# A planned two-stage kernel: scalar loads behind a pair's values, three loads in halves, a weight cast on GpSimd, and a new order

## The chip, the core and the metric

The kernel runs on one core of a Trainium2 chip. The core has TensorE (PE), which multiplies matrices out of SBUF into PSUM, VectorE (DVE), ScalarE (ACT), GpSimd (POOL) and SyncE (SP). Each takes its instructions in the order in which the program gave them; SP's queue here holds nothing but transfers. The metric is the time of one execution on the device in microseconds (us), as the median of several runs; less is better.

## What is computed

Two stages follow each other. The first is a gated linear recurrence over 768 steps, for 4 batches of 8 heads of width 48:

```
for t in range(S):
    state = alpha[:, :, t, :, None] * state + einsum('bhd,bhe->bhde', k[:, :, t], v[:, :, t])
    y[:, :, t] = einsum('bhd,bhde->bhe', q[:, :, t], state)
```

Its output, laid out as x with 3072 rows of 384, goes through a two-layer network with 2048 hidden columns:

```
h = x @ w_in;  r = maximum(h, 0);  g = s * (r * r) + b;  out = g @ w_out
```

s and b are single numbers. All inputs and the output are float32; the kernel multiplies in bf16. Since b is the same for every hidden column, its part of the output is one row (b times the column sums of w_out), computed once as bias_w.

## The kernel before

**Blocks.** The 768 steps of each batch are cut into 6 blocks of 128, 24 blocks in all (n = 0 to 23). The first four are worked as two *pairs*, whose two blocks are loaded interleaved into space that later holds hidden activations (gt); each other block has its own a, q, k and v tile, in five slots (`n % NIN`). The chain of a block: load alpha, q, k, v (192 KB each; `load`, L225); logarithm of alpha on ACT (L381; pairs L552); cumulative sum as a matmul with a triangle of ones (L387, L394; pairs L559, L569); exponentials of it and of its negative on ACT (L403, L406; pairs L578, L583); q times the first and k times the second on DVE (L417, L422; pairs L590); both transposed, for pairs by PE (L605) with a copy out of PSUM by DVE (L616), for later blocks by a transposing transfer that ACT issues (`st_Tdma`, L439); A, the matmul of the two (L490); the causal mask on DVE (L499); y out of A, v and the state (L528); y evacuated by ACT into xd (L673). Beside it the state: v cast to bf16 on POOL (L411; pairs L621), KV (L448; pairs L655), the state's sum on DVE (L469, L473), its decay on POOL (L484). For a pair, half of each block's values lies on the wrong 64 partitions; PE shifts them (L631) and two copies per pair put them in place (`pair_vcopy`, L644).

**The network.** Blocks are taken in groups of one or two (GROUPS). A unit is a piece of the first layer that fills one PSUM bank (mm1, L693: 6 matmuls of 256 columns or 12 of 128, w_in as weights), then relu on ACT (L702) and a square on DVE into gt (L708). A quad is four of the sixteen matmuls that make a block's output (mm2, L755). The last quad of a block is followed by `oevac` on DVE (L766: times s, plus bias_w) and the output store (`ostore`, L779).

**Weights.** w_in and w_out come in four parts each of 768 KB (L310, L333), are cast to bf16 by the engine that the list CE names (L319 on ACT, L321 on DVE, L323 on POOL), and DVE sums w_out's columns (L343, L348, L351). b and s are loaded by POOL (`load_bs`, L359, L360); b is first read by `bias_mul` (L363, "bones"), s by `oevac`.

**What sets the order.** Nothing is ordered by hand and nothing by the framework: the class Schedule holds every operation with its engine, a guessed duration, a priority and what it reads and writes, plays them through once while the program is built, and emits them in the order in which they begin there. On each engine, among the operations that are ready, the one with the least priority value goes first; P holds one offset for each kind of operation, UNIT and LEAD turn a block's number into a base. LOADS gives the order of the first transfers in SP's queue. [...] FILL matmuls on zeros (L1028) are put where this play leaves PE idle before the first quad. So one constant changed can move any instruction on any engine; the hardware keeps the order, and waits by semaphores for what an instruction reads.

Of the kernel before, what the change touches and what calls it, by code (L numbers as in the profile page):

```python
# [14 lines left out]

VW = 144

GROUPS = [2, 2, 1, 1, 1, 1, 2, 2, 2, 2, 2, 2, 2, 2]
UNIT = 0.392
LEAD = {1: 204.6, 2: 323.1, 4: 100.0}  # L20

NPE = 4

NAY = 12

# [6 lines left out]
TP = 1.45  # L32
LATE = 2.5
NY = 2
NKV = 7
NR2 = 2
STQ = 18
TC2 = ["DVE", "DVE"]
VC2 = ["ACT", "ACT"]
CE = ["POOL", "DVE", "ACT", "ACT", "ACT", "ACT", "ACT", "ACT"]  # L40
TC = dict(ACT=1.4, DVE=0.87, POOL=2.0)
FILL_GAP = 0.2
COLD = 9.0

P_BM, P_CS, P_BMM = -5, -286.4, 473.5
P = dict(
    ln=34.88, cum=-15.29, eb=-32.24, ei=9.49, vc=73.43, qb=-9.65, kb=14.71, T=95.62,
    Tc=-13.62, KV=-13.54, t1=9.55, sn=124.73, Ay=-11.39, A=-22.53, mk=-58.68, y=-13.83,
    ye=5.65, m1=-19.67, re=9.86, sq=-33.02, m2=-18.25, oe=-24.3, vm=-57.17, ci=324.52,
    co=-825.8, ls=148.33, vn=-450.01,  # L50
)

LOADS = ["V0", "i0", "A0", "K0", "Q0", "A1", "V1", "Q1", "i1", "K1", "i2", "i3", "v4", "o0", "o1", "o2", "o3", "a4", "k4", "q4"]

class Schedule:
    HOP = 0.05
# [90 lines left out]
def kernel(  # L147
# [12 lines left out]
    nc = tc.nc  # L160
    ctx.enter_context(tc.manual_schedule())

    B, H, S, D = q.shape
    C = 128
# [7 lines left out]
    NIN = 5  # L172
# [31 lines left out]
    a_in = many("a_in", NIN, [128, H, D], FP32)  # L204
# [17 lines left out]

    def load(n, src, dst):
        b, c = n // NCH, n % NCH
        nc.sync.dma_start(  # L225
            out=dst[n % NIN],
            in_=src[b, :, c * C : (c + 1) * C, :].rearrange("h s d -> s h d"),
        )

    for x, src in enumerate((alpha, q, k, v)):  # L230
        load_pair(0, x, src)
# [62 lines left out]
    out_sb = many("o_sb", 3, [128, d_model], FP32)  # L294
# [368 lines left out]
    blk_group = []  # L663
    for g, m in enumerate(GROUPS):
        blk_group += [(g, t) for t in range(m)]
# [11 lines left out]
    quads = []  # L677
    for g, m in enumerate(GROUPS):
        per = 4 // m
        for u in range(NJ // per):  # L680
            units.append((g, [u * per + i for i in range(per)]))
        for tt in range(m):
            for jq in range(NJ // 4):
                quads.append((g, tt, jq))
    first_blk = [sum(GROUPS[:g]) for g in range(len(GROUPS))]

    def mm1(w):
        g, js = units[w]
        n = GROUPS[g] * C
        hp = h_ps[w % 2]  # L690
# [126 lines left out]
    for rank, item in enumerate(loads):  # L817
        t, i = rank - 1000, int(item[1:])
        if item[0] in "AQKV":
            if i == 1:  # L820
                load_pair_op(item[0], i)
            continue
        if item[0] in "aqkv":
            if i < N1 + NIN:
                load_op(item[0], i)
            continue
        st = stage
        stage += 1
        key = [("wst", st)]
        if st >= NST:  # L830
            h = (st - NST) // 2 % 2
            key = [("gt", x, j) for x in range(9 - 3 * h, 12 - 3 * h) for j in range(NJ)]
            key = key[24 * (st % 2) : 24 * (st % 2) + 24] + [("wst", st)]
        if st >= NST:
            reuse.append((len(sched.ops), [(x, h) for x in ("AQ", "KV")[st % 2]]))
        eng = CE[st]
        if item[0] == "i":
            op("SP", TW, t, load_w_in, i, st, w=key, lat=2.0)
            op(eng, TC[eng], P["ci"], cast_w_in, i, st, eng, r=key, w=[("wib", i)], lock=eng != "ACT")
        else:  # L840
            op("SP", TW, t, load_w_out, i, st, w=key, lat=2.0)
            op(eng, TC[eng], P["co"], cast_w_out, i, st, eng, r=key, w=[("wob", i)], lock=eng != "ACT")
# [12 lines left out]
    def pb(n):  # L855
        return "ct" if n >= NKV else "py"

# [106 lines left out]
    def add_group(g):  # L964
        nonlocal unit_i, quad_i
        if g == 0:
            op("PE", 0.65, P_BMM, bias_mm, r=["bones", "colsum"], w=[("o", 0)], lat=0.16)
            op("DVE", 0.53, -300, bias_copy, r=[("o", 0)], w=["bias"])
        m = GROUPS[g]
        ring = [(first_blk[g] + x) % RING for x in range(m)]  # L970
        per = 4 // m
        for u in range(NJ // per):
            w = unit_i
            unit_i += 1
            js = units[w][1]
            t = w * UNIT
            op("PE", {1: 0.67, 2: 0.656, 4: 0.648}[m], t + P["m1"], mm1, w,
               r=[("xd", g % 3, x) for x in range(m)] + [("wib", js[0] // 4)],
               w=[("h", w % 2)], lat=0.16)
            op("ACT", 0.52, t + P["re"], relu, w, r=[("h", w % 2)], w=[("r", w % 2)])  # L980
            op("DVE", 0.345, t + P["sq"], square, w, r=[("r", w % 2)],
               w=[("gt", x, j) for j in js for x in ring], lock=True)
        for u in range(4 * m):
            x = quad_i
            quad_i += 1
            tt, jq = quads[x][1:]
            if x >= len(quads) - 4:
                continue
            ob = (x // 4) % 2
            t = (x + 4 * m + P["m2"]) * UNIT  # L990
            op("PE", 0.65, t, mm2, x,
               r=[("gt", ring[tt], j) for j in range(4 * jq, 4 * jq + 4)] + [("wob", jq)],
               w=[("o", ob)], lat=0.16)
# [69 lines left out]
```

## Time and profile before

| | us |
|---|---|
| median of 7 runs (186.11 to 188.29) | 186.62 |
| the profiled execution's own time | 187.21 |
| its span, first to last instruction | 185.4 |
| busy in the span: PE, DVE, ACT, POOL | 174.0, 135.0, 106.4, 39.5 |
| groups: mm1 matmuls (672), mm2 matmuls (368) | 74.4, 69.4 |
| groups: relu (96), squares (96), masks (24) | 55.4, 42.5, 29.3 |

The profiled execution is one of the seven, 0.6 us above their median; 1.8 us of it lie outside the span. The mean granted clock of PE is 0.991 of full. The DMA engines move 35.48 MB, most of it in packets under 512 bytes, and are full nearly throughout the first three quarters of the span. A busy PE is not the same as a PE at its peak, since the ends of matmuls are modelled and overlap; so what PE waits for is read from its idle time and from what ended it.

### The profile page before, as it was taken

The numbers are of one execution on the slowest core, as the hardware profiler recorded it, in microseconds if no ns is written. First come the engines' busy times: TensorE is split into PE (matmuls) and PEld (weight loads), VectorE is DVE, ScalarE is ACT, GpSimd is POOL, SyncE is SP. The second block draws the span as 40 slices with busy tenths as digits, with TensorE's granted clock in tenths as the row PEclk, the third lists the DMA queues.
The fourth block names the chain that finished last, engine by engine and source line by source line (L and its number), as shares of the span: only waits on it lengthen the run. The fifth ranks groups of instructions, "written<-read, shape, count | busy, mean of one in ns | idle before, by whom it ended". The sixth has DMA issues, their size and how long they took to land.

```text
span 185.4 us, 5345 instructions
## 1 busy us (share of the span) xinstructions
PE 174.0 (94%) x2149; PEld 124.0 (67%) x2151; DVE 135.0 (73%) x251; ACT 106.4 (57%) x215; POOL 39.5 (21%) x71
## 2 busy tenths in 40 slices
PE   6878987999999999999989999999999899999993
PEld 2346764766877667776667776787777677777562
DVE  2389999899498778769769986879788586554321
ACT  3437898874637555675257666585648365665000
POOL 7994032031012221211203230100232130010000
PEclk9999997999999999999999999999999999999999
DMA  5999998999999999999999999799997983000122
GB/s 155 355 315 368 354 378 242 202 193 223 215 193 202 186 160 276 175 219 221 226 183 241 170 226 216 173 203 166 237 142 160 182 172 66 0 11 34 54 77 85
DMA packets 119961, 35.48 MB, mean 191 GB/s; under 512 B 113232, under 2 KB 118352, under 8 KB 119936
## 3 DMA queue, kind: packets, MB, share of 16 engines
q1 hardware_dynamic: 98688, 29.70, 71.2%
q10 hardware_dynamic: 21120, 5.25, 20.8%
q8 instruction: 17, 0.28, 0.7%
q0 software_dynamic: 128, 0.20, 0.3%
q14 instruction: 8, 0.07, 0.1%
HBM read 25.17 MB, written 4.72 MB: 161 GB/s over the span
## 4 chain that ended last, share of the span: by engine, by line
PE 55%; DMA 17%; DVE 16%; issue 4%; ACT 3%; SPq 1%; POOL 1%; ACTq 1%; DVEq 0%; POOLq 0%
PE h_ps L693 21%; PE o_ps L755 21%; DMA v_in<-in_v_dram 9%; DMA qkT<-qk 3%; PE py_ps L528 3%; DVE gt L708 3%; DVE am L499 3%; DMA out_dram<-o_sb 3%; PE a_ps L490 3%; DMA gt<-in_alpha_dram 2%; DVE colpart L343 2%; DVE o_sb L766 2%; ACT r L702 2%; DVE s_st L473 1%; DVE qk L422 1%
## 5 line engine op out<-in xcount | busy, mean ns | idle before, releaser
L693 PE MATMUL h_ps<-xd,w_in_bf 128*128 128x256 bf16 (+1 forms) x672 | 74.4, 260 | 0.8 <-ACT r L702 0.8
L702 ACT ACTIVATE r<-h_ps 128x512 bf16<-128x512 f32 x96 | 55.4, 601 | 29.9 <-PE h_ps L693 11.7
L755 PE MATMUL o_ps<-w_out_bf,gt 128*128 128x384 bf16 x368 | 69.4, 328 | 1.4 <-ACT w_out_bf L319 1.3
L693 PEld LDWEIGHTS <-w_in_bf 128*128 128x128 bf16 x672 | 56.7, 98 | 11.4 <-issue 1.6
L708 DVE TENSOR_TENSOR gt<-r 128x512 bf16<-128x512 bf16 x96 | 42.5, 458 | 15.9 <-ACT r L702 15.4
L755 PEld LDWEIGHTS <-gt 128*128 128x128 bf16 x368 | 34.4, 98 | 20.4 <-issue 1.7
L499 DVE TENSOR_TENSOR am<-a_ps,mask 128x1024 bf16<-128x1024 f32 x24 | 29.3, 1220 | 3.1 <-PE a_ps L490 2.8
L411 POOL CAST vp<-v_in 128x384 bf16<-128x384 f32 x20 | 11.5, 575 | 68.2 <-DMA v_in<-in_v_dram 62.8
L484 POOL TENSOR_TENSOR s_st<-s_st,blast 128x384 bf16<-128x384 bf16 x16 | 14.0, 874 | 43.0 <-DVE s_st L473 30.9
L766 DVE SCALAR_TENSOR_TENSOR o_sb<-o_ps,s_col,bias_w 128x384 f32<-128x384 f32 x23 | 14.2, 616 | 8.8 <-PE o_ps L755 7.9
L673 ACT ACTIVATE xd<-py_ps 128x384 bf16<-128x384 f32 x22 | 11.1, 503 | 12.4 <-PE py_ps L528 12.3
L381 ACT ACTIVATE la<-a_in 128x384 bf16<-128x384 f32 x20 | 10.5, 524 | 7.8 <-DMA a_in<-in_alpha_dram 3.1
L417 DVE TENSOR_TENSOR qk<-q_in,b_s 128x384 bf16<-128x384 f32 x20 | 12.6, 632 | 2.6 <-DMA q_in<-in_q_dram 1.6
L473 DVE TENSOR_TENSOR s_st<-ct_ps,s_st 64x192 bf16<-64x192 f32 x24 | 8.5, 354 | 7.0 <-PE ct_ps L448 4.3
L403 ACT ACTIVATE b_s<-ct_ps 128x384 f32<-128x384 f32 x20 | 9.8, 491 | 5.5 <-PE ct_ps L394 3.9
L422 DVE TENSOR_TENSOR qk<-k_in,binv 128x384 bf16<-128x384 f32 x20 | 11.0, 549 | 0.4 <-DMA k_in<-in_k_dram 0.4
L490 PE MATMUL a_ps<-qkT 64*128 64x128 bf16 x192 | 9.5, 218 | 1.5 <-DMA qkT<-qk 0.8
L490 PEld LDWEIGHTS <-qkT 64*128 64x128 bf16 x192 | 5.6, 94 | 7.7 <-issue 5.4
L406 ACT ACTIVATE binv<-ct_ps 128x384 f32<-128x384 f32 x20 | 9.9, 494 | 0.0
L1028 PE MATMUL o_ps<-zeros 128*128 128x512 bf16 x19 | 7.7, 550 | 1.3 <-DVE zeros L236 1.3
L528 PE MATMUL py_ps<-am,vp 128*32 128x128 bf16 x352 | 8.8, 219 | 0.0
L528 PEld LDWEIGHTS <-vp 128*32 128x32 bf16 x384 | 6.5, 97 | 0.7 <-issue 0.3
(93 smaller groups left out, 124.5 us busy)
## 6 DMA issues: line engine op xcount, KB each, us to landing
out_dram<-o_sb SPq DMA_DIRECT2D x22, 192.0 KB, 3.3
v_in<-in_v_dram SPq DMA_DIRECT2D x20, 192.0 KB, 4.6
a_in<-in_alpha_dram SPq DMA_DIRECT2D x20, 192.0 KB, 4.5
k_in<-in_k_dram SPq DMA_DIRECT2D x20, 192.0 KB, 4.9
q_in<-in_q_dram SPq DMA_DIRECT2D x20, 192.0 KB, 4.7
wst<-in_moe_w_in_dram SPq DMA_DIRECT2D x4, 768.0 KB, 7.1
gt<-in_moe_w_out_dram SPq DMA_DIRECT2D x4, 768.0 KB, 10.0
gt<-in_alpha_dram SPq DMA_DIRECT2D x2, 384.0 KB, 4.6
```

The source lines that it names most:

```text
L411: nc.gpsimd.tensor_copy(out=vp_sb[n % 4].rearrange("a p (x d) -> a p x d", d=D)[:, :, 0:3:2, :], in_=v_in[n % NIN].rearrange("a (p e) d -> ...
L417: nc.vector.tensor_tensor(out=qk_sb[n % 4][:, 0, :, 0:D], in0=q_in[n % NIN], in1=b_sb[n % 2], op=ALU.mult)
L422: nc.vector.tensor_tensor(out=qk_sb[n % 4][:, 1, :, 0:D], in0=k_in[n % NIN], in1=binv_sb[n % 2], op=ALU.mult,)
L484: nc.gpsimd.tensor_tensor(out=s_sb[n % 3], in0=t1_sb[n % 2], in1=bl, op=ALU.mult)
L490: nc.tensor.matmul(out=a_ps[:, e, p, :], lhsT=qkT[64 * e : 64 * e + 64, 1, p, :], rhs=qkT[64 * e : 64 * e + 64, 0, p, :], start=True, stop ...
L499: nc.vector.tensor_tensor(out=am_sb[n % 2].rearrange("a e p t -> a (e p) t"), in0=a_ps.rearrange("a e p t -> a (e p) t"), in1=(mask2 if n ...
L528: nc.tensor.matmul(out=y_of(n)[32 * (x % 4) : 32 * (x % 4) + 32, x // 4, :], lhsT=(st[:, p, c0 : c0 + 32] if e is None else vp[:, p, c0 + ...
L693: nc.tensor.matmul(out=hp[:, i * n : (i + 1) * n], lhsT=w_in_bf[:, kk, 128 * j : 128 * (j + 1)], rhs=xd_sb[g % 3][:, kk, 0:n], start=(kk = ...
L702: nc.scalar.activation(out=r_sb[w % 2], in_=h_ps[w % 2], func=AF.Relu)
L708: nc.vector.tensor_tensor(out=gt_sb[:, s0 : s0 + m, js[0] : js[0] + len(js)].rearrange("a s j t -> a j s t"), in0=r, in1=r, op=ALU.mult,)
L755: nc.tensor.matmul(out=op[:, 0:d_model], lhsT=gt_sb[:, s0, j], rhs=w_out_bf[:, j, :], start=(j == 0), stop=(j == NJ - 1),)
L766: nc.vector.scalar_tensor_tensor(out=ots, in0=o_ps[(x // 4) % 2][:, 0:d_model], scalar=s_col, in1=bias_w, op0=ALU.mult, op1=ALU.add,)
```

## The change

1. For the planner `load_bs` now reads ("V", 1) as well. In the emitted order POOL's two small loads come behind the four value casts of the second pair; before they stood ahead of the first pair's.
2. `load` takes q, k and v of block 20 in two transfers of four heads (96 KB) each.
3. CE: the first w_in part is cast by ACT (was POOL), the fourth by POOL (was ACT); the second stays with DVE.
4. VC2: all four copies of `pair_vcopy` go to DVE (were on ACT).
5. STQ is gone: block 18's output store is issued by SP like the others (was POOL).
6. LOADS: k4 comes ahead of the last two w_in parts, v4 between w_out's second and third part (v4 was ahead of all of w_out, k4 behind it).
7. [...] The groups of one are now blocks 4, 5, 8 and 11 (were 4, 5, 6 and 7); NKV = 8 puts KV of block 7 in the bank that y uses (was ct). NPE decides nothing, since blocks below 4 are pairs.

Counted in the emitted order, the matmuls are the same but for the filling ones, 28 for 21. DVE has the four copies more, ACT has them less; POOL has one store less, SP one store and three loads more.

```
-GROUPS = [2, 2, 1, 1, 1, 1, 2, 2, 2, 2, 2, 2, 2, 2]
-UNIT = 0.392
-LEAD = {1: 204.6, 2: 323.1, 4: 100.0}
+GROUPS = [2, 2, 1, 1, 2, 1, 2, 1, 2, 2, 2, 2, 2, 2]
+UNIT = 1.077
+LEAD = {1: 168.0, 2: 386.1, 4: 142.5}
...
-NKV = 7
+NKV = 8
...
-STQ = 18
-VC2 = ["ACT", "ACT"]
-CE = ["POOL", "DVE", "ACT", "ACT", "ACT", "ACT", "ACT", "ACT"]
-TC = dict(ACT=1.4, DVE=0.87, POOL=2.0)
+VC2 = ["DVE", "DVE"]
+CE = ["ACT", "DVE", "ACT", "POOL", "ACT", "ACT", "ACT", "ACT"]
+TC = dict(ACT=1.43, DVE=1.7, POOL=1.44)
...
-LOADS = ["V0", "i0", "A0", "K0", "Q0", "A1", "V1", "Q1", "i1", "K1", "i2", "i3", "v4", "o0", "o1", "o2", "o3", "a4", "k4", "q4"]
+LOADS = ["i0", "K0", "V0", "A0", "Q0", "A1", "V1", "Q1", "i1", "K1", "k4", "i2", "i3", "o0", "o1", "v4", "o2", "o3", "a4", "q4"]
...
-        nc.sync.dma_start(
-            out=dst[n % NIN],
-            in_=src[b, :, c * C : (c + 1) * C, :].rearrange("h s d -> s h d"),
-        )
+        parts = 2 if n == 20 and dst is not a_in else 1
+        for x in range(parts):
+            hs = slice(H // parts * x, H // parts * (x + 1))
+            nc.sync.dma_start(
+                out=dst[n % NIN][:, hs],
+                in_=src[b, hs, c * C : (c + 1) * C, :].rearrange("h s d -> s h d"),
+            )
...
-        eng = nc.gpsimd if n == STQ else nc.sync
-        eng.dma_start(out=out[n * C : (n + 1) * C, :], in_=out_sb[(x // 4) % 3])
+        nc.sync.dma_start(out=out[n * C : (n + 1) * C, :], in_=out_sb[(x // 4) % 3])
...
-    op("POOL", 1.3, P["ls"], load_bs, w=["b", "s"], lat=3.5)
+    op("POOL", 1.3, P["ls"], load_bs, r=[("V", 1)], w=["b", "s"], lat=3.5)
```

More of the change, by code (lines that the diff above doesn't have):

```diff
@@ L16 @@
 VW = 144
-GROUPS = [2, 2, 1, 1, 1, 1, 2, 2, 2, 2, 2, 2, 2, 2]
-UNIT = 0.392
-LEAD = {1: 204.6, 2: 323.1, 4: 100.0}
-NPE = 4
+GROUPS = [2, 2, 1, 1, 2, 1, 2, 1, 2, 2, 2, 2, 2, 2]
+UNIT = 1.077
+LEAD = {1: 168.0, 2: 386.1, 4: 142.5}
+NPE = 3
 NAY = 12
@@ L34 @@
 NY = 2
-NKV = 7
+NKV = 8
 NR2 = 2
-STQ = 18
 TC2 = ["DVE", "DVE"]
-VC2 = ["ACT", "ACT"]
-CE = ["POOL", "DVE", "ACT", "ACT", "ACT", "ACT", "ACT", "ACT"]
-TC = dict(ACT=1.4, DVE=0.87, POOL=2.0)
+VC2 = ["DVE", "DVE"]
+CE = ["ACT", "DVE", "ACT", "POOL", "ACT", "ACT", "ACT", "ACT"]
+TC = dict(ACT=1.43, DVE=1.7, POOL=1.44)
 FILL_GAP = 0.2
 COLD = 9.0
-P_BM, P_CS, P_BMM = -5, -286.4, 473.5
+P_BM, P_CS, P_BMM = -5, -325.9, 395.8
 P = dict(
[L47 to L50, printed above, removed]
+    ln=35.49, cum=-10.85, eb=-37.47, ei=4.86, vc=55.25, qb=-19.41, kb=-10.54, T=88.06,
+    Tc=0.54, KV=-11.01, t1=-10.95, sn=133.44, Ay=-8.08, A=-21.08, mk=-45.88, y=-14.78,
+    ye=21.19, m1=-23.61, re=10.04, sq=-36.78, m2=-8.37, oe=-2.45, vm=-57.61, ci=558.48,
+    co=-752.06, ls=340.37, vn=-303.05,
 )
-LOADS = ["V0", "i0", "A0", "K0", "Q0", "A1", "V1", "Q1", "i1", "K1", "i2", "i3", "v4", "o0", "o1", "o2", "o3", "a4", "k4", "q4"]
+LOADS = ["i0", "K0", "V0", "A0", "Q0", "A1", "V1", "Q1", "i1", "K1", "k4", "i2", "i3", "o0", "o1", "v4", "o2", "o3", "a4", "q4"]
 class Schedule:
@@ L838 @@
             op("SP", TW, t, load_w_in, i, st, w=key, lat=2.0)
-            op(eng, TC[eng], P["ci"], cast_w_in, i, st, eng, r=key, w=[("wib", i)], lock=eng != "ACT")
+            op(eng, TC[eng], P["ci"], cast_w_in, i, st, eng, r=key, w=[("wib", i)], lock=eng == "POOL")
         else:
             op("SP", TW, t, load_w_out, i, st, w=key, lat=2.0)
-            op(eng, TC[eng], P["co"], cast_w_out, i, st, eng, r=key, w=[("wob", i)], lock=eng != "ACT")
+            op(eng, TC[eng], P["co"], cast_w_out, i, st, eng, r=key, w=[("wob", i)], lock=eng == "POOL")
             op("DVE", 0.88, P_CS, colsum_part, i, st, r=key,
@@ L976, in add_group @@
             t = w * UNIT
-            op("PE", {1: 0.67, 2: 0.656, 4: 0.648}[m], t + P["m1"], mm1, w,
+            op("PE", {1: 0.675, 2: 0.66, 4: 0.652}[m], t + P["m1"], mm1, w,
                r=[("xd", g % 3, x) for x in range(m)] + [("wib", js[0] // 4)],
@@ L990, in add_group @@
             t = (x + 4 * m + P["m2"]) * UNIT
-            op("PE", 0.65, t, mm2, x,
+            op("PE", 0.655, t, mm2, x,
                r=[("gt", ring[tt], j) for j in range(4 * jq, 4 * jq + 4)] + [("wob", jq)],
```

## The prediction

> **What bounds the kernel now.** I read the page's engine shares first, then its slices, then the busy time by stretch, then TensorE's waits in order of time, then the single instructions between 8 and 45 us.
>
> ```profile
> PE 174.0 (94%) x2149; PEld 124.0 (67%) x2151; DVE 135.0 (73%) x251; ACT 106.4 (57%) x215; POOL 39.5 (21%) x71
> ...
> PE   6878987999999999999989999999999899999993
> ...
> PEclk9999997999999999999999999999999999999999
> DMA  5999998999999999999999999799997983000122
> ```
>
> TensorE (PE) is busy 94% of the span. Its low digits stand in the first seven slices (to 32 us); after that it is full. So a change can pay or cost in two places: in the start, where PE waits for others, and in the few waits later on.
>
> ```profile
> 10.00:15.00 5.00, 4.03 (x66) 2.69 (x68) 4.38 (x9) 2.04 (x4) 4.64 (x8) 1.00 1.11 332
> 15.00:20.00 5.00, 4.50 (x62) 3.19 (x63) 4.83 (x6) 4.36 (x9) 1.05 (x2) 1.00 1.07 374
> 20.00:25.00 5.00, 4.93 (x90) 3.88 (x88) 4.67 (x10) 4.49 (x6) 1.08 (x2) 1.00 1.09 347
> 25.00:30.00 5.00, 3.57 (x54) 2.56 (x54) 4.96 (x8) 5.00 (x7) 1.41 (x2) 0.97 1.07 367
> 30.00:35.00 5.00, 5.00 (x30) 3.40 (x28) 4.34 (x8) 3.69 (x5) 0.00 (x0) 0.68 0.79 159
> ```
>
> Columns: stretch and length, then busy time of PE, PEld, DVE, ACT, POOL, then granted clock, DMA share, GB/s. VectorE (DVE) is full from 10 to 30 us (4.4 to 5.0 of 5), ScalarE (ACT) from 15 to 30. The start is a race between DVE's queue and the arrival of the weights.
>
> ```profile
> 51.66 0.40 PE L490 MATMUL a_ps<-qkT 64*128 64x128 bf16 x8 [0.24 <-DVE am L499]
> 60.93 0.40 PE L490 MATMUL a_ps<-qkT 64*128 64x128 bf16 x8 [0.36 <-DMA qkT<-qk]
> 65.34 0.33 PE L448 MATMUL ct_ps<-vp,qk 128*128 128x96 bf16 x4 [0.39 <-POOL vp L411]
> 96.95 0.82 PE L693 MATMUL h_ps<-xd,w_in_bf 128*128 128x256 bf16 x6 [0.80 <-ACT r L702]
> 109.29 0.40 PE L490 MATMUL a_ps<-qkT 64*128 64x128 bf16 x8 [0.42 <-DMA qkT<-qk]
> 147.34 0.33 PE L448 MATMUL ct_ps<-vp,qk 128*128 128x96 bf16 x4 [0.69 <-POOL vp L411]
> ```
>
> In brackets stands the idle time before the group and what ended it. From 36 to 182 us these six are all of PE's waits: 2.9 us. That is the most that a better order can win there; the matmuls themselves stay (four groups of one block and ten of two in both kernels).
>
> **The start.** The change moves the four pair copies of L644 (two per pair) from ACT to DVE, ahead of everything else that DVE does for the second pair.
>
> ```profile
> 11.31 0.99 ACT L644 ACTIVATE vp<-o_ps 64x384 bf16<-64x384 f32 x2 [2.91 <-PE o_ps L631]
> ...
> 11.83 0.74 DVE L469 TENSOR_TENSOR s_st<-py_ps,blast 64x192 bf16<-64x192 f32 x2
> ...
> 21.24 0.68 DVE L616 COPY qkT<-py_ps 128x1024 bf16<-128x1024 bf16 x1
> ...
> 21.98 0.23 PEld L490 LDWEIGHTS <-qkT 64*128 64x128 bf16 x8 [0.45 <-DVE qkT L616]
> ...
> 22.42 1.22 DVE L499 TENSOR_TENSOR am<-a_ps,mask 128x1024 bf16<-128x1024 f32 x1 [0.17 <-PE a_ps L490]
> ```
>
> PE's first matmul on block 2 (21.98) waits for DVE's copy that ends at 21.92, and from 10.56 to there DVE's instructions sum to 11.6 us in 11.4 us: no gap in which four more could hide. DVE has no such copy in this trace. From below, a 64x192 operation out of PSUM takes 0.352 us, though it moves half as much; from above, the bias copy of 384 columns takes 0.556.
>
> ```profile
> L473 DVE TENSOR_TENSOR s_st<-py_ps,s_st x6: 339/352/361, 13.7 to 27.8; 64x192 bf16<-64x192 f32 x6
> ...
> L377 DVE COPY bias_w<-o_ps x1: 556/556/556, 38.6 to 38.6; 128x384 f32<-128x384 f32 x1
> ```
>
> It has 384 columns, like the latter, so I take 0.53 each: 2.1 us in all, bounds 1.4 and 2.2. The bias product (0.57) moves from before the second pair's products to after them, but still stands ahead of the qkT copies, so it gives nothing back.
>
> Followed through the new order with these durations: qkT copies of pair 0 end at 11.84 as now; two copies to 12.9; mask 0 to 14.12; state product to 14.86; mask 1 to 16.08; two copies to 17.1; state sums to 17.85; w_in cast to 19.6; the second pair's products to 21.5 (now 19.88); two squares and the bias product to 22.8; qkT copies to 24.15 (now 21.92); two squares; mask 2 from 24.95 (now 22.42). Mask 3 then ends at 28.5 (now 25.98). The new order puts w_out's first two column sums (0.95 each) and a square ahead of block 3's state sum, which ends at 31.6 (now 28.16), and y of block 3, which overwrites the bank that the sum reads, starts there (now 28.21). ACT then evacuates y to 32.75 and casts the third w_out part to 34.25, the fourth, behind one relu, to 36.35 (now 35.43). PE issues the fourth w_out quad at 36.4 (now 35.48) with one mm1 unit (0.655) fewer behind it. At the end of the three quads after KV of block 4 the new order stands at 42.95 with 14 units done; now it is 41.36 with 15. The lag is 1.6 + 0.65 = **2.3 us**. With 0.352 per copy it is 1.5.
>
> Four more edits lie in the start. *The w_in cast on GpSimd* (POOL) takes 1.46 (its row at 11.62); the part lands at about 23.2 (now 22.0, plus 1.2 for block 4's k load now ahead of it: v4 landed 1.2 after the part before it), so it is cast by 24.7, and its readers start at 27.2. Hidden from PE; but POOL and DVE hold each other up:
>
> ```profile
> 28.30 1.00 POOL L484 TENSOR_TENSOR s_st<-s_st,blast 128x384 bf16<-128x384 bf16 x1 [2.88 <-DVE s_st L473]
> ...
> 28.53 1.58 DVE L343 TENSOR_TENSOR colpart<-gt 128x768 f32<-128x768 f32 x1
> ```
>
> The same sum takes 0.95 alone, the POOL product 0.83. The square due at 24.15 may wait for the cast's end: 0 to 0.5 us more lag; I take 0, since the part may land half a us earlier. [...]
>
> *b and s behind the second pair's values*: 0.69 + 0.54 us of POOL at 7.5 move to about 14.7, and land 4.8 us later, near 20.2; the bias product stands at 22.3, s is read first at 41. The first pair's casts start up to 0.7 earlier (its values land at 8.0, the casts begin at 8.73), but the shift matmuls that read them stand behind PE's transposes (10.89): nothing. If b came 2 us later still, DVE's queue would stop for it. *v4 between the w_out parts* makes the last two land up to 1.2 later, near 30.7 and 33.5; their casts wait longer for ACT than that. *Seven more filling matmuls* (21 to 28, 0.22 each) stand in waits of 1.8 and 2.1 us: hidden.
>
> The clock: it was 0.50 from 29.9 to 33.3 though no PE gap there exceeds 0.85 us, and two units took 2.64 instead of 1.3. [...] By the row it may run at half clock again. I leave it out of the sum: PE waits for ACT's casts until 36.4 either way; at half clock up to 0.7 us more stays.
>
> **The later part.** v loads wait in SP's queue behind output stores. At 140.33 DVE evacuates block 15, the store is issued at 140.98, v22 at 141.90, lands 4.76 later, is cast by 147.28: about 7.9 us of PE's work, where the order holds 7.2. Counting matmuls (unit 0.655, quad 0.65, A 0.33, y 0.5) between that quad and KV 22, the new order holds 9.6: the wait of 0.69 goes. Likewise v9: 10.5 held, 10.9 needed, 11.1 held now: 0.39 goes. The tightest new one is v19 with 8.6. The halved loads of block 20 add three issues of about 0.45 us to SP, with 14.3 us between the store they follow and KV 20: nothing, and at worst 1.4 us out of 6.4 spare. Block 18's store, back on SP, comes after all loads: nothing. For the other four waits (1.82) the distance from a block's cumulative sum to its A is 8.1 to 10.2 us before (A7 13.6) and 8.2 to 10.3 after (A7 13.2): unchanged; they may all go, or as much may come. The later part gives **-1.1 us**, bounds -2.9 and +0.7.
>
> **Sum.** 2.3 - 1.1 = +1.2 on the span of 185.4: 186.6, and with the 1.8 us that lie outside it (187.21 - 185.4) 188.4 for an execution like the profiled one. That one is 0.6 above the median, 186.62, so the forecast is **187.8 us**.
>
> **Rivals.**
> *Faster.* The mechanism is the later order: all six waits go (-2.9), and the DVE copies cost 0.352, so the lag is 1.5: -1.4, 185.2 us. It decides where the lag falls below what the order saves. For it: two waits are accounted for, and the waits for transposes shrink if PE itself comes later. Against it: the nearer copy row.
> *Even.* A lag of 1.5 and 1.1 to 1.5 saved: 186.6 to 187.0. The w_out transfers, which do not move before the second part, would then set the pace in both.
> *Much slower.* The lag of 2.3, plus 0.5 for the POOL cast, and nothing saved because new waits (v19, A14 or A16) replace the old: +2.8, 189.4.
>
> **Chances.** Forecast case 0.33, faster 0.31, even 0.16, much slower 0.20. About 0.5% (0.93 us) is what a measurement can tell from no change: faster means below 185.7, slower above 187.55. The forecast case lies mostly above (0.27 of 0.33), so slower 0.47, same 0.22, faster 0.31. The range from 184.9 to 189.4 leaves out the ends of the first and last rivals; the forecast's own is 187.2 to 188.6.
>
> **What would show it.** Right: DVE copies near 0.53 us in the L644 group, mask of block 2 near 25 us, y of block 3 near 31.6, the fourth w_out cast ending after 36, no PE wait for v22. Wrong: mask 2 before 23.5, or w_out's casts at their old times; then the start costs nothing and the time falls with the waits. If PE idles over 3 us after 45 us, the order made new waits.

## The result, and the profile after

Side by side on one chip the changed kernel takes 187.79 us (median of 27 runs), the kernel before 186.27 (64 runs): ratio 1.0084, interval 1.0063 to 1.0104. It is slower by 0.8%. The ratio and its interval leave out executions more than 1.5% above the fastest of their kernel, and both profiled executions are among those; the medians hold all. The forecast was 187.8 against a median of 186.62, which is +0.63%. The number was right; that it fits so closely is partly luck, since against the median measured beside it the change is +1.5 us, and +1.2 was forecast. The working behind it was right in the sign and the path of its first term, and partly wrong in what makes it; its second term is within what one execution differs from the next.

The profiled execution of the changed kernel took 189.37 us, with a span of 187.7 and a mean granted clock of 0.990. It is 1.6 us above its own median, where the one before is 0.9 above the 186.27; so the two spans lie 2.3 us apart and the medians only 1.5. What follows divides the 2.3.

First the page of the changed kernel: engine shares, then PE, granted clock and DMA over 40 slices of 4.7 us.

```profile
PE 175.8 (94%) x2156; PEld 124.7 (66%) x2158; DVE 136.5 (73%) x255; ACT 104.3 (56%) x211; POOL 41.2 (22%) x70
...
PE   6987987989999999899999899999999999999993
...
PEclk9997899999999999999999999999999999999999
DMA  5998999799999999999999999999979971101122
```

The low digits of PE now reach into the ninth slice (37.5 to 42.2 us; before, the seventh), and the clock's drop has moved from the seventh slice to the fourth and fifth. The same stretches of the start as in the prediction, in the same columns:

```profile
10.00:15.00 5.00, 4.14 (x64) 2.52 (x64) 4.62 (x8) 2.53 (x3) 3.01 (x7) 1.00 1.05 319
15.00:20.00 5.00, 3.95 (x54) 2.50 (x52) 4.25 (x6) 1.63 (x4) 2.12 (x4) 0.68 0.84 201
20.00:25.00 5.00, 4.95 (x45) 3.60 (x44) 3.99 (x8) 4.17 (x8) 0.08 (x1) 0.98 1.02 332
25.00:30.00 5.00, 3.93 (x72) 3.16 (x72) 4.92 (x7) 3.40 (x5) 2.64 (x2) 1.00 1.10 359
30.00:35.00 5.00, 3.65 (x56) 2.55 (x55) 4.90 (x8) 3.65 (x5) 2.54 (x2) 1.00 1.07 314
```

Two rows matter. From 15 to 20 us the DMA moves 201 GB/s (before: 374), so the weights come later. From 30 to 35 PE is busy for 3.65 us of 5 (before: all 5), so the start now ends after 35.

PE's waits from 15 us to the end, idle time and what ended it in brackets:

```profile
16.41 0.35 PE L633 MATMUL ct_ps<-vc,ident_bf 64*64 64x384 bf16 x1 [1.05 <-DVE vp L648]
28.11 0.40 PE L492 MATMUL a_ps<-qkT 64*128 64x128 bf16 x8 [0.84 <-DVE am L501]
28.75 0.35 PE L530 MATMUL py_ps<-qkT,s_st 128*32 128x128 bf16 x12 [0.23 <-DVE s_st L475]
33.18 0.35 PE L530 MATMUL py_ps<-qkT,s_st 128*32 128x128 bf16 x12 [1.35 <-DVE s_st L475]
38.07 0.81 PE L757 MATMUL o_ps<-w_out_bf,gt 128*128 128x384 bf16 x4 [0.56 <-DVE colpart L345]
75.88 0.81 PE L695 MATMUL h_ps<-xd,w_in_bf 128*128 128x256 bf16 x6 [1.12 <-ACT r L704]
103.79 0.40 PE L492 MATMUL a_ps<-qkT 64*128 64x128 bf16 x8 [0.54 <-DMA qkT<-qk]
```

Behind 40 us only the last two are left, 1.66 us; before there were six, 2.90 us. The waits for the casts of v9 and v22 are gone. Since PE is full otherwise, the span splits in two: *later waits* W (all waits behind the three quads that follow KV of block 4, at about 42 us), and *start* S, which is span less W. That is 182.5 + 2.9 = 185.4 before and 186.0 + 1.7 = 187.7 after. So in these two executions the start costs **+3.5 us** (forecast +2.3), and the later part gives **1.2 back** (forecast 1.1).

How far one execution can be trusted for this, the profiles of the experiments below show. Four of them run the same instructions as one of the two kernels until the three quads are under way. These end at 41.16 (e7), 42.13 (e8) and 42.20 us (e11) where the kernel before has 41.52, and at 43.80 (e5) where the changed one has 44.31. With one mm1 unit (0.65) on top, the start costs between 2.3 and 3.8 us. W moves more: ahead of 140 us, where its edit lies, e8 waits 1.22 us and the kernel before 2.21, mostly at other places; and e10, the changed kernel but for three small edits, waits 3.48 where the changed kernel waits 1.66. So the 1.2 given back are not told from nothing by two profiles.

Where this execution's 3.5 come from: the three quads end at 44.31 (41.52 before), with one mm1 unit (0.65) fewer behind them. Single instructions of DVE, of the changed kernel, in order:

```profile
11.59 1.12 DVE L648 CAST vp<-o_ps 64x384 bf16<-64x384 f32 x2
...
15.79 0.56 DVE L648 CAST vp<-ct_ps 64x384 bf16<-64x384 f32 x1
16.79 0.55 DVE L648 CAST vp<-ct_ps 64x384 bf16<-64x384 f32 x1 [0.44 <-PE ct_ps L633]
...
23.70 0.69 DVE L618 COPY qkT<-ct_ps 128x1024 bf16<-128x1024 bf16 x1 [0.90 <-PE ct_ps L607]
...
24.91 2.02 DVE L710 TENSOR_TENSOR gt<-r 128x512 bf16<-128x512 bf16 x2
26.85 1.21 DVE L501 TENSOR_TENSOR am<-a_ps,mask 128x1024 bf16<-128x1024 f32 x1
```

The copies take 0.56 each (forecast 0.53). Three things were not in the forecast. DVE waits 0.44 us for the second shift matmul, which itself waits (16.41, 1.05) for the first copy out of the same bank: a chain that ACT's copies did not make DVE stand in. Other work is shorter than forecast and makes this up: the bias product ends at 22.81, where the forecast had 22.8. Next, DVE waits 0.90 us for PE's transposes (23.70), so that the qkT copies end at 24.99 instead of 24.15. PE is late by then: it idled the 1.05, and ran at half clock from 16.8 to 20.2. In e9, with the same copies and the same wait of 1.05 but no drop of the clock, the transposes start at 21.81 instead of 23.06, and DVE does not wait for them. Last, a square takes 1.68 us where the median of the five from 20 to 30 us is 0.42, beside POOL's w_in cast:

```profile
24.92 1.72 POOL L325 CAST w_in_bf<-wst 128x1536 bf16<-128x1536 f32 x1 [5.92 <-DMA wst<-in_moe_w_in_dram]
```

```profile
L710 DVE TENSOR_TENSOR gt<-r x5: 417/418/1684, 21.9 to 28.7; 128x512 bf16<-128x512 bf16 x5
```

The second view gives minimum, median and maximum in ns of the squares from 20 to 30 us. Mask 2 therefore starts at 26.85, not 24.95. From there the forecast's path holds, each step late: block 3's state sum ends at 33.13 (forecast 31.6), ACT has evacuated y by 34.41 (32.75), and the last two w_out casts follow:

```profile
34.27 1.47 ACT L321 ACTIVATE w_out_bf<-gt 128x1536 bf16<-128x1536 f32 x1
...
36.54 1.48 ACT L321 ACTIVATE w_out_bf<-gt 128x1536 bf16<-128x1536 f32 x1
```

The second ends at 38.02 (36.35), and the fourth quad, which reads what it casts, starts at 38.07 (36.4). The view of PE's waits names DVE's column sum there, which ended at 38.03; but the quad does not read the column sum.

The transfers moved too. SyncE's queue, kernel before first, then the changed one: the last two w_in parts, and parts of w_out.

```profile
11.88 1.79 SPq L310 DMA_DIRECT2D wst<-in_moe_w_in_dram  x2
```

```profile
13.23 5.10 SPq L312 DMA_DIRECT2D wst<-in_moe_w_in_dram  x2
...
21.10 6.58 SPq L335 DMA_DIRECT2D gt<-in_moe_w_out_dram  x2
```

The third w_in part (384 rows of 2 KB) stands behind the second pair's last loads and block 4's k (1024 rows or more each, and under way): its issue lasts 4.33 us, and the fourth goes out at 17.60. From 16.8 to 19.0 the DMA has run dry and moves 64 to 179 GB/s. The w_out parts then land at 27.2, 29.4, 33.8 and 35.9 (before: 25.3, 27.4, 30.2 and 32.3); the last two casts start 0.5 and 0.6 us behind their parts.

Of the experiments' profiled executions, e7's lies 1.2 us and e10's 1.8 us above its kernel's median; the others lie within about 0.5 of theirs.

### The profile page after: what moved, and what is told of

It is laid out like the page before. It is cut to its first block, busy times and chain, and to the rows that moved or that the text cites. A ratio compares the mean times of both kernels' runs of the same rounds, so it can differ in the third digit from the quotient of the medians.

```text
span 187.7 us, 5367 instructions
## 1 busy us (share of the span) xinstructions
PE 175.8 (94%) x2156; PEld 124.7 (66%) x2158; DVE 136.5 (73%) x255; ACT 104.3 (56%) x211; POOL 41.2 (22%) x70
## 2 busy tenths in 40 slices
DMA packets 120089, 35.48 MB, mean 189 GB/s; under 512 B 113280, under 2 KB 118528, under 8 KB 120064
## 3 DMA queue, kind: packets, MB, share of 16 engines
q10 hardware_dynamic: 21120, 5.25, 20.2%
## 4 chain that ended last, share of the span: by engine, by line
PE 62%; DMA 16%; DVE 14%; issue 4%; ACT 1%; ACTq 0%; POOL 0%; SPq 0%; POOLq 0%
PE o_ps L757 25%; PE h_ps L695 23%; DMA qkT<-qk 7%; PE py_ps L530 4%; DMA v_in<-in_v_dram 4%; DMA a_in<-in_alpha_dram 3%; PE a_ps L492 3%; DVE am L501 2%; DVE gt L710 2%; DMA gt<-in_alpha_dram 2%; PE a_ps L561 2%; DVE colpart L345 1%; DVE qkT L618 1%; PE ct_ps L389 1%; DVE qk L424 1%
## 5 line engine op out<-in xcount | busy, mean ns | idle before, releaser
L695 PE MATMUL h_ps<-xd,w_in_bf 128*128 128x256 bf16 (+1 forms) x672 | 73.5, 258 | 1.3 <-ACT r L704 1.1
L704 ACT ACTIVATE r<-h_ps 128x512 bf16<-128x512 f32 x96 | 55.9, 601 | 33.8 <-PE h_ps L695 15.3
L486 POOL TENSOR_TENSOR s_st<-s_st,blast 128x384 bf16<-128x384 bf16 x16 | 15.3, 957 | 51.2 <-DVE s_st L475 28.7
L419 DVE TENSOR_TENSOR qk<-q_in,b_s 128x384 bf16<-128x384 f32 x20 | 11.1, 554 | 3.3 <-ACT b_s L405 3.0
L424 DVE TENSOR_TENSOR qk<-k_in,binv 128x384 bf16<-128x384 f32 x20 | 12.5, 627 | 0.0
L1029 PE MATMUL o_ps<-zeros 128*128 128x512 bf16 x26 | 9.2, 504 | 1.5 <-DVE zeros L238 1.3
L475 DVE TENSOR_TENSOR s_st<-ct_ps,s_st 64x192 bf16<-64x192 f32 x22 | 7.7, 352 | 1.7 <-PE ct_ps L450 1.4
L530 PE MATMUL py_ps<-qkT,s_st 128*32 128x128 bf16 x228 | 6.7, 222 | 1.6 <-DVE s_st L475 1.6
```

The costliest lines, as they stand in the source:

```text
L419: nc.vector.tensor_tensor(out=qk_sb[n % 4][:, 0, :, 0:D], in0=q_in[n % NIN], in1=b_sb[n % 2], op=ALU.mult)
L424: nc.vector.tensor_tensor(out=qk_sb[n % 4][:, 1, :, 0:D], in0=k_in[n % NIN], in1=binv_sb[n % 2], op=ALU.mult,)
L486: nc.gpsimd.tensor_tensor(out=s_sb[n % 3], in0=t1_sb[n % 2], in1=bl, op=ALU.mult)
L530: nc.tensor.matmul(out=y_of(n)[32 * (x % 4) : 32 * (x % 4) + 32, x // 4, :], lhsT=(st[:, p, c0 : c0 + 32] if e is None else vp[:, p, c0 + ...
L695: nc.tensor.matmul(out=hp[:, i * n : (i + 1) * n], lhsT=w_in_bf[:, kk, 128 * j : 128 * (j + 1)], rhs=xd_sb[g % 3][:, kk, 0:n], start=(kk = ...
L704: nc.scalar.activation(out=r_sb[w % 2], in_=h_ps[w % 2], func=AF.Relu)
```

## The experiments

Two theories at first. *Q*: DVE's queue (four copies, the held square) sets the start, and the start sets the end. *T*: the landings of the weights set it. After the first four runs both had fallen, and a third took their place, *P*: transfers are full from the start to about 105 us (the DMA row of the changed kernel's page has 9 in 20 of its first 23 slices, and 5, 8 and 7 in the others), so a start that is gained or lost is given back in later waits for transfers; with rival *O*: those waits come from the order alone. e9 asks whether the edits at the start or the new order cost the time (*E* against *O*).

All kernels but e9 keep the planner's order of the kernel they start from, apart from the instructions named. S and W are worked out as above, from one profile each; the ratio is to the kernel before on the same chip, whose medians were 186.89 (e1 to e4), 186.81 (e5 to e8) and 187.01 us (e9 to e12). The changed kernel was not run again beside them, so its 1.0084 comes from another session. S also holds all of PE's work behind the start, and any drop of the clock.

| kernel | us | ratio (interval) | span | S | W |
|---|---|---|---|---|---|
| before | 186.27 | 1 | 185.4 | 182.5 | 2.90 |
| after | 187.79 | 1.0084 (1.0063, 1.0104) | 187.7 | 186.0 | 1.66 |
| e1 after, copies and w_in cast on ACT | 189.29 | 1.0125 (1.006, 1.0189) | 187.8 | 185.2 | 2.59 |
| e2 after, first loads as before | 189.03 | 1.0108 (1.0043, 1.0172) | 186.8 | 185.8 | 1.02 |
| e3 after, both | 189.68 | 1.0157 (1.0102, 1.0213) | 188.2 | 183.8 | 4.45 |
| e4 before, copies on DVE | 187.25 | 1.0032 (0.9994, 1.007) | 186.0 | 185.0 | 0.98 |
| e5 after, fewer loads | 188.94 | 1.0115 (1.008, 1.0151) | 187.3 | 185.4 | 1.92 |
| e6 e3, fewer loads | 188.49 | 1.0052 (1.0011, 1.0094) | 186.8 | 185.0 | 1.85 |
| e7 before, fewer loads | 185.02 | 0.9936 (0.9907, 0.9965) | 184.5 | 182.2 | 2.28 |
| e8 before, store 15 later | 185.90 | 0.9919 (0.988, 0.9959) | 184.2 | 183.0 | 1.22 |
| e9 edits, old planning numbers | 189.85 | 1.0143 (1.0085, 1.02) | 187.9 | 184.9 | 3.02 |
| e10 after, small edits undone | 188.94 | 1.0067 (1.0022, 1.0112) | 189.0 | 185.5 | 3.48 |
| e11 before, eight stores later | 189.34 | 1.0114 (1.0051, 1.0177) | 187.7 | 185.1 | 2.58 |
| e12 after, w_in cast on ACT | 189.40 | 1.0113 (1.0072, 1.0155) | 187.5 | 185.2 | 2.35 |

**e1: the copies and the fourth w_in cast back on ACT.**

```
-op(..., cast_w_in, i, st, eng, ...)
+op(..., cast_w_in, i, st, "ACT" if i == 3 else eng, ...)
-op(..., pair_vcopy, m, c, eng, ...)
+op(..., pair_vcopy, m, c, "ACT", ...)
```

> The changed kernel in its own order, but the four pair copies and the fourth w_in cast are issued to ACT (DVE and POOL lose them). Theory Q (DVE's queue sets the lag of the start, as predicted): DVE loses 2.2 us of copies and the 1.26 us by which a square was held up beside the POOL cast, mask 2 comes near 23.7 instead of 26.85, and about 2.6 us go: ratio to the kernel before near 0.994. Rival T (the weights' transfers set it: in the changed kernel the third and fourth w_out part land near 33.8 and 35.9, 3.6 us later than before, because block 4's k load now stands ahead of them): those landings stay, the fourth cast still ends near 37.5, at most 0.7 us go: ratio 1.004 or above.

The start gained only 0.8 us (S 186.0 to 185.2), and the time nothing. PE's waits of e1:

```profile
37.97 0.81 PE L757 MATMUL o_ps<-w_out_bf,gt 128*128 128x384 bf16 x4 [0.67 <-ACT w_out_bf L321]
64.09 0.40 PE L492 MATMUL a_ps<-qkT 64*128 64x128 bf16 x8 [1.36 <-DMA qkT<-qk]
86.53 0.40 PE L492 MATMUL a_ps<-qkT 64*128 64x128 bf16 x8 [0.35 <-DMA qkT<-qk]
103.63 0.40 PE L492 MATMUL a_ps<-qkT 64*128 64x128 bf16 x8 [0.47 <-DMA qkT<-qk]
112.83 0.40 PE L492 MATMUL a_ps<-qkT 64*128 64x128 bf16 x8 [0.41 <-DMA qkT<-qk]
```

The fourth w_out quad stays at 37.97 (38.07): its cast now waits for the part that lands at 36.4. So with DVE relieved the landings hold the start, and what is gained goes into waits for transposes. Q alone falls.

**e2: the first loads in their old places** (v4 ahead of w_out, k4 behind a4).

```
+put(at(load, 4, v), at(load_w_out, 0), 0)
+put(at(load, 4, k), at(load, 4, alpha), 1)
```

> The changed kernel in its own order on all engines but SP, where k4 goes back behind a4 and v4 ahead of w_out. Theory Q: y of block 3 still waits for DVE until 33, so the third cast still starts near 34: at most 0.4 us go, ratio 1.006 or above. Rival T: w_out's parts land near 25.3, 27.3, 29.5 and 32.3 again and 1.0 to 1.9 us go: ratio 0.998 to 1.003. Both theories: no dip of the transfers at 15 to 18 us (228 GB/s in the changed kernel).

The fourth quad stands at 38.41 and S is 185.8. The w_out parts do not come back to their old times (28.3, 30.4, 32.5 and 34.6), but the landings are not the limit here: the fourth cast starts 2.3 us behind its part, since y of block 3 waits for DVE until 33.5. T alone falls as well: the two limits stand side by side, and taking one away shows the other.

**e3: both together.**

> Both at once: the changed kernel's order, copies and fourth w_in cast on ACT, first transfers as before. If the start then costs what it cost before, only the gain of the later part stays (1.66 us of PE waits after 36 us instead of 2.9): ratio near 0.993. If one of the two theories is the whole cause, this run equals the run that undoes that cause alone; if both are needed, it is lower than either by over 0.5 us.

Now the start is short: the fourth quad at 35.65, as in the kernel before (35.48), and S down by 2.3. Yet the ratio is 1.0157, where 0.993 was expected, the highest of the four. PE's waits behind the start:

```profile
42.31 0.32 PE L389 MATMUL ct_ps<-la,U_bf 128*128 128x384 bf16 x1 [0.41 <-ACT binv L408]
48.86 0.32 PE L389 MATMUL ct_ps<-la,U_bf 128*128 128x384 bf16 x1 [1.13 <-ACT la L383]
64.10 0.40 PE L492 MATMUL a_ps<-qkT 64*128 64x128 bf16 x8 [1.60 <-DMA qkT<-qk]
82.34 0.83 PE L695 MATMUL h_ps<-xd,w_in_bf 128*128 128x128 bf16 x12 [0.44 <-ACT r L704]
104.45 0.40 PE L492 MATMUL a_ps<-qkT 64*128 64x128 bf16 x8 [0.87 <-DMA qkT<-qk]
```

The 1.13 us are a wait for block 7's alpha, landing 6.1 us after its issue; the 1.60 a transpose that was issued at 56.50 and took 7.55 us (5.96 in the changed kernel, issued at 57.07). A of block 14 comes between 102.6 and 104.5 us in the changed kernel and in all those made from it in its order, wherever their start ended. This is where theory P comes from.

**e4: the kernel before with its four copies on DVE.**

```
-op(..., pair_vcopy, m, c, eng, ...)
+op(..., pair_vcopy, m, c, "DVE", ...)
```

> The kernel before in its own order, only the four pair copies issued to DVE. Theory Q: DVE has no gap from 10.6 to 22, so its 2.2 us reach mask 2 (22.42 to about 24.5) and most of them the end: +1.5 to +2.2 us, ratio 1.008 to 1.012. Rival T: PE waits for w_out's landings anyway (0.47 and 0.85 us idle at 27 and 29), so at most +0.6: ratio 1.003 or below.

The start is 2.5 us longer, where the four copies were costed at 2.1; part of it may be the granted clock, which was at half from 14.0 to 20.9 us in this execution. In place of six later waits there are three short ones, 0.98 us. The time rises by 0.3% only, not told from none. The likely reason, which this run alone does not show, is that a lag which PE brings along lets the transfers catch up.

**e5 and e6: fewer loads.** Eleven loads of v are left out; e5 starts from the changed kernel, e6 from e3. The first of them would go out at 60 us (59.50 in e3), not at 42 as the expectations say, so what differs ahead of that is not their doing.

```
+        if dst is v_in and 9 <= n < 20:
+            return
```

> The changed kernel with the 11 loads of v for blocks 9 to 19 left out (these blocks reuse an older v, so their outputs are not the reference's); every other instruction and its order stay. This takes 192 KB out of each 768 KB that a block loads from about 42 us on, a quarter of the loads. Theory P (transfers set the pace between 40 and 105 us, so that an earlier start is given back to waits for transposes): the one PE wait for a transpose (0.54 at 103.8) goes and nothing else, since this kernel waited only 1.66 us in all after the start; the start's lag stays: span near 187.0, ratio to before about 1.005. Theories Q and T (the start's lag alone makes the 2.3 us): the same within 0.6, so 187.0 to 187.7; this kernel is the base for the next one.

> The kernel with the copies and the fourth w_in cast back on ACT and the first loads in their old places, again with the 11 loads of v for blocks 9 to 19 left out (their outputs are not the reference's). It had its fourth w_out group 2.4 us earlier than the changed kernel, and waited 4.45 us later on, 2.5 of it for two transposes and 1.1 for a load of alpha. Theory P: with fewer transfers in flight these 3.6 us go, the early start comes through, and the span falls from 188.2 to about 184.5, 2.5 below the changed kernel with the same loads left out. Rival O (the waits come from the order, which was laid out for a later start, and not from how full the transfers are): the waits stay but for 1 us at most, and the span stays above 187.0, no lower than the changed kernel with the same loads left out.

PE's waits of e6 behind the start:

```profile
44.11 0.32 PE L391 MATMUL ct_ps<-la,U_bf 128*128 128x384 bf16 x1 [0.77 <-ACT binv L410]
102.89 0.40 PE L494 MATMUL a_ps<-qkT 64*128 64x128 bf16 x8 [1.08 <-DMA qkT<-qk]
```

P holds in part. The ratio falls from 1.0157 to 1.0052, by 2.0 us, with intervals that do not meet; by the medians of all executions it falls from 1.0149 to 1.0090, by 1.1 us. So there is a gain, but its size is open, while the changed kernel gains nothing from the same cut (1.0115). Block 7's transpose, issued at 56.70, takes 6.2 us instead of e3's 7.55, and PE does not wait for it. But the span is 186.8, not 184.5. The wait for block 14's transpose stays (1.08; 0.89 in e5), which points to the order: block 14's cumulative sum stands 8.4 us of work ahead of its A, against 9.6 in the kernel before. And the start of this execution was 1.2 us longer than e3's, with the clock at half from 31.5 to 35.0 us. That the wait at 48.86 is gone is not the doing of the missing loads, since nothing was left out so early.

**e7: the kernel before with the same loads left out.**

> The kernel before, with the 11 loads of v for blocks 9 to 19 left out (their outputs are not the reference's). Its waits after the start are 2.9 us: 0.8 for two transposes, 1.1 for two casts of v (of blocks 9 and 22), 0.8 for a ReLU, 0.2 for a mask. Theory P: the transposes' 0.8 and the 0.39 of the cast of v 9 go, the 0.69 of v 22 stays: span near 184.2. Rival O: only the 0.39 goes, span near 185.0. In both, the distance to the changed kernel with the same loads left out is the start's lag with the other waits: 2 to 3 us.

Both waits for transposes go, and v22's falls to 0.33, but a wait of 1.50 for block 6's logarithm comes at 42.66, ahead of the first missing load (about 58 us). The span of 184.5 lies between the two expectations; the ratio is 0.9936. The distance to e5 is 2.8 us of span, within the 2 to 3 expected, and 3.3 us by the two ratios. With all loads the two kernels lie 1.5 us apart. The starts of these two executions lie 3.3 us apart (43.80 and 41.16 at the three quads, and one unit). So with fewer loads the whole lag of the start seems to reach the end, which speaks for P.

**e8: the kernel before with block 15's store behind k22 and v22.**

```
+put(at(ostore, 63), at(load, 22, v), 1)
```

> The kernel before, with one output store (block 15's) issued behind the loads of k and v of block 22 in SyncE's queue instead of ahead of them. The recorded prediction puts PE's wait of 0.69 us for the cast of v 22 down to this store: by it the wait goes and the span falls to about 184.7, ratio 0.996, unless PE then meets another wait. If the wait was set by the transfer itself and not by the place in the queue, nothing changes: 185.4.

The wait for v22 goes, as the prediction read it. Of PE's later waits these are left:

```profile
61.78 1.50 PE L693 MATMUL h_ps<-xd,w_in_bf 128*128 128x128 bf16 x24 [0.30 <-ACT r L702]
71.10 0.40 PE L490 MATMUL a_ps<-qkT 64*128 64x128 bf16 x8 [0.51 <-DMA qkT<-qk]
108.90 0.40 PE L490 MATMUL a_ps<-qkT 64*128 64x128 bf16 x8 [0.41 <-DMA qkT<-qk]
```

At 185.90 us (0.9919) this kernel beats both. Of the 1.2 us of span, the edit accounts for 0.69; the rest lies in other waits of a single execution and is not traced to it.

**e9: all edits, with the planning numbers of the kernel before.** GROUPS, UNIT, LEAD, NPE, NKV and P, all of which the change sets anew, are the old ones, and the planner orders the rest from those; TC, the guessed durations of mm1 and mm2 and the casts marked `lock` (the planner lets no two operations with this mark overlap) stay new.

> All the edits of the change (copies on DVE, w_in casts, first loads, b and s, halves, store 18), but the planner's numbers of the kernel before (groups, unit, leads, weights of the steps), so that the rest of the work is ordered from those. Theory E (the edits at the start cost the time): the block of quads behind KV 4 ends 2.5 us or more later than in the kernel before, the later waits take back about 1, ratio 1.0075 or more. Theory O (the new order costs the time, and the edits only shift the start, which the later waits take back as in the kernel before with copies on DVE, 1.0032): ratio 1.005 or less.

Theory E, in the time: 1.0143. The start is 2.4 us longer, and here W gives nothing back: after 41 us PE waits 1.69 us for two logarithms, which wait for the loads of alpha, and 1.33 for ReLUs. The 1.69 are landings of loads again, in the other order and at another place.

**e10: three small edits undone**: b and s loaded ahead of the first pair's casts, block 20 loaded whole, store 18 on POOL.

```
-parts = 2 if n == 20 and dst is not a_in else 1
+parts = 1
+eng = nc.gpsimd if n == 18 else nc.sync
+put(at(load_bs), <POOL's first operation>, 0)
```

> The changed kernel with three small edits undone in its own order: the loads of b and s issued ahead of the first pair's casts on GpSimd, block 20's loads whole, block 18's store on GpSimd's queue. The recorded prediction costs all three at nothing: ratio to before as the changed kernel's, 1.0084, within 0.003; span 187.7. If the two issues (0.70 and 0.54 at 15.05 on GpSimd) or the three added issues on SyncE cost after all, the ratio falls below 1.005.

1.0067, and its interval takes in 1.0084: no difference that can be told, as forecast.

**e11: the kernel before with eight stores behind the loads that they stood ahead of.**

```
+for n, m in ((0, 7), (1, 7), (3, 9), (5, 11), (6, 13), (12, 19), (13, 21), (15, 22)):
+    put(at(ostore, 4 * n + 3), at(load, m, v), 1)
```

> The kernel before with eight output stores (blocks 0, 1, 3, 5, 6, 12, 13 and 15) issued behind the loads of k and v that they stood ahead of. With block 15's alone the ratio was 0.9919. If each store that waits ahead of loads costs something: below 0.990, span under 184. If only the store ahead of v 22 mattered: 0.992, 184.2. If loads that come earlier hold up the transposes (5 to 7 us each): waits for transposes come in, and the ratio is 0.996 or more.

The third expectation holds in the time and in one wait. SyncE no longer waits for those eight results before it loads, and block 10's transpose, issued at 71.97, comes 7.2 us later:

```profile
75.85 1.49 PE L693 MATMUL h_ps<-xd,w_in_bf 128*128 128x256 bf16 x12
79.17 0.40 PE L490 MATMUL a_ps<-qkT 64*128 64x128 bf16 x8 [1.83 <-DMA qkT<-qk]
79.50 0.82 PE L755 MATMUL o_ps<-w_out_bf,gt 128*128 128x384 bf16 x4
80.16 2.53 PE L693 MATMUL h_ps<-xd,w_in_bf 128*128 128x256 bf16 x12
```

The same 12 matmuls take 1.49 us before the wait and 2.53 after it: the granted clock fell from 1.00 to 0.50. With 0.70, 0.50, 0.50 and 0.60 granted in the four microseconds from 80, PE loses about 1.7 us (an estimate, the sum of what is missing to 1.00), which stand in this kernel's S (185.1); another 0.7 is there before the first moved store would have gone out (41.56): the three quads start at 40.09 instead of 39.41. W as a whole is no greater than before (2.58 against 2.90). So the loss is measured, and one wait of it seen, but how the eight stores make the 1.1% is not settled.

**e12: the fourth w_in cast alone on ACT.** The edit is the first half of e1's.

> The changed kernel with the fourth w_in cast on ACT instead of GpSimd, all else in its order. In the changed kernel the square beside this cast took 1.68 us in place of 0.42. If DVE's queue sets the start, the square's 1.26 comes back: fourth w_out group near 36.8 instead of 38.1, span near 186.5, ratio near 1.002. If the landings of the w_out parts set it, or ACT's queue now does (the cast is 1.4 us of ACT ahead of the w_out casts): the fourth group stays within 0.5 of 38.1 and the ratio within 0.003 of 1.0084.

The square's loss is gone: mask 2 starts at 25.86 instead of 26.85, and S is 0.9 less. But the fourth quad only comes to 37.48, since its cast now waits for the part that lands at 35.9, and the time is not shorter (1.0113). W is 0.7 more, which two profiles do not tell from none. The cast on POOL cost a square 1.26 us in the start, and the time nothing that can be told.

## Why the prediction was right, and where it was not

- **The start, "the lag is 1.6 + 0.65 = 2.3 us".** Right in sign and in its path (state sum, y, casts, fourth quad), too small for the profiled execution: 2.8 + 0.65 at the three quads, 3.5 in S. Over all profiles with either start it is 2.3 to 3.8. The copies were sized well (0.56 for 0.53). Missed were the held square and DVE's wait of 0.90 for PE's transposes. In the latter the clock has a part, which the forecast left out of its sum, and so have three of the filling matmuls that it called hidden: they stand on PE ahead of the unit at 21.75 (0.65). Mask 2 came at 26.85 instead of 25, y of block 3 at 33.18 instead of 31.6.
- **The cast on POOL, "I take 0".** This step failed. The prediction had bounded the loss at 0 to 0.5 and hoped for an early landing; the part landed at 24.9, 1.7 later than taken, and the cast met the square: +1.26 (1.68 for 0.42). The square (25.24 to 26.92) began 0.32 behind the cast (24.92 to 26.64) and ended 0.28 behind it; in e12, with the cast on ACT, no square from 20 to 30 us takes more than 0.43. e12 also shows that in this kernel the time does not feel it (1.0113).
- **The loads, "last two land up to 1.2 later".** This step failed. k4 ahead of the last w_in parts let SyncE's queue stand for over 4 us, and the four w_out parts land 1.9, 1.9, 3.6 and 3.6 later. (The third part's old landing, taken as 29.5, is 30.2.) The rival "even" leaned on the same view ("do not move before the second part") and was wrong with it. The forecast's reason ("their casts wait longer for ACT than that") still held in the changed kernel, whose casts start 0.5 and 0.6 behind their parts, but only because DVE was later than forecast: in e1 and e12 the last cast waits for its part.
- **The later part, "-1.1 us".** Measured -1.24, in one execution of each kernel. v22's wait went by the reason given: none of the eight profiles in the new order has it, and e8 takes it away by moving the one store. For v9's the reason is not shown: it is gone in e8 too, 75 us ahead of that edit. The other four waits (1.82) are gone as well, and two at other places (a ReLU, block 14's transpose) make up 1.66. With 3.48 in e10, that the sum fits is chance.
- **b and s, block 20 in halves, store 18: nothing.** Not contradicted (e10).
- **The rivals.** "Much slower" had a lag of 2.8 and nothing saved; the profile's lag is larger still, but the time is 187.8 and not 189.4. "Faster" needed copies of 0.352; they take 0.56.
- **What the forecast treated as a sum is not one.** It added a lag in the start to a saving later on. The runs show that the two are coupled: in the old order the copies add 2.5 to S and W loses 1.9 (e4); in the new order the edits undone take 2.3 from S and add 2.8 to W (e3). These are single profiles, but the times agree: e4 is 0.3% slower and not 0.8 to 1.2%, and e3 is not faster than the changed kernel at all. The accounting "start +3.5, later -1.2" holds for the two profiled executions; that the copies or the loads *cause* the 0.8% is not shown, since no undoing of them in the new order made it faster.

So the cause is settled in part. That the start is longer, and that DVE's queue and the landings hold it side by side, is shown (e1, e2, e3). What makes 0.8% of the time out of it is not. The edits in the old plan cost 1.4% (e9), the new order without the edits of the start 1.6% (e3), both together 0.8%: it looks as if each fits the other, but the intervals of e9 and e3 begin at 1.0085 and 1.0102, where the changed kernel's ends at 1.0104. That full transfers give back part of a start is supported by e3 against e6 (1.1 to 2.0 us) and by e5 against e7; e6's wait for block 14 suggests that the order counts too. The clock is a rival that no run rules out (last section). Which part of the new order costs the rest was not tried. Of the kernels in the changed kernel's order only e3 and e6 are told apart by their intervals; e1, e2, e5, e10 and e12 are not told from the changed kernel itself.

## What to carry to other kernels

Split a span into the start and the later waits before adding up terms: a lag in the start is worth only what the later waits do not give back, and undoing one of two limits that stand side by side shows only the other. Profile more than one execution before you subtract two spans: here the waits behind the start differed by 1 to 1.8 us with the same or nearly the same instructions. Where transfers were full here, a load that went out earlier could be paid for by another: one store moved behind two loads gained 0.8%, eight lost 1.1%. Before a cast goes to POOL, look for DVE's instructions beside it (here a square of 0.42 took 1.68), and count with where the transfers will land in the new order, not with where they landed (here w_out's parts came 1.9 to 3.6 us later).

## What the runs showed of the hardware

- **Stretches of half clock came behind some waits and not behind others.** In e11, PE was idle from 77.34 to 79.17; the granted clock of the microseconds from 80 on was 0.70, 0.50, 0.50, 0.60, then 1.00 again. In the changed kernel it was at half from 16.8 to 20.2, behind the wait of 1.05 at 16.41; in e2, e5 and e12 the same stretch came with the same wait, beginning within 0.8 us of its end. In e9 none came with it, nor behind the waits of 1.60 in e3 and 1.50 in e7. Four of the profiled executions (e1, e3, e7, e9; mean clock 1.000) show no such stretch, the others 3.4 or 6.8 us of it (mean clock 0.990 or 0.991, and 0.981 or 0.982). Of the changed kernel's 28 executions, the 20 with a mean clock of 0.991 or less have a median of 188.1 us, the others 187.3; of the 64 of the kernel before that ran beside the experiments, the 28 with such a clock have 187.0, the others 186.7. How much of the 0.8% is the clock stays open.
- **The issue of a short transfer stood behind long ones.** In the changed kernel the issue of a w_in part of 384 rows lasted 4.33 us behind loads of 1024 rows or more (0.72 to 1.15 for the others), and when those were done the DMA had little to do (64 GB/s) till it was through. With block 4's k back behind it the same issue lasted 1.1 us (e2, e3).
- **Transposes were quicker with fewer loads.** From issue to landing they took 3.4 to 6.9 us in the changed kernel, up to 7.6 in e3. With the loads of v left out, the median from 60 to 84 us, of four or five transfers each, was 4.2 instead of 4.9 in the kernel before, 5.2 instead of 5.8 in the changed one and 5.0 instead of 5.9 in e3.
